# Order of TensorE's stages in a planned kernel: small-tile stages in bundles between token products

## The chip, the cores and the metric

The kernel runs on one core of a Trainium2 chip. The metric is device time in microseconds of one execution, the median of 3 runs. A core has five engines with a queue of their own each: TensorE (PE; its weight loads are shown as PEld), VectorE (DVE), ScalarE (ACT), GpSimd (POOL) and SyncE (SP), which here only issues the DMA transfers. They wait for one another by semaphores, and each works through its own instructions in the order in which the program has them.

## The reference, cut to what matters

Four batches, 8 heads, 576 positions, head size 64, 32 memory slots; all in float32. An attention over a memory is followed by a mixture of 4 experts with given shares, and that by a soft mixture of 8 experts with 4 slots each.

```python
# attention over memory, per batch and head
a = softmax(phi, axis=memory)                    # [576, 32]
k_m, v_m = a.T @ k, a.T @ v                      # [32, 64]
x = softmax(q @ k_m.T / 8) @ v_m                 # [576, 64], heads side by side: [2304, 512]

# first mixture: N 2304, D 512, E 4, F 1024
p = domain_probs / domain_probs.sum(-1)
x = sum(p[:, e:e+1] * (relu(x @ w1[e]) @ w2[e]) for e in range(4))

# second mixture: 8 experts, 32 slots in all
logits = x @ phi2                                # [2304, 32]
d = softmax(logits, axis=0)                      # over all tokens
slot_input = (d.T @ x).reshape(8, 4, 512)
slot_out[e] = relu(slot_input[e] @ v1[e]) @ v2[e]
out = softmax(logits, axis=1) @ slot_out         # [2304, 512]
```

## The kernel before, in words

**What it computes in place of x.** The kernel never makes the attention's output or the first mixture's output. With the 256 attention weights of a token (8 heads, 32 slots) called A, `x @ w1[e]` is `A @ (v_m @ w1[e])`. So for each batch and each chunk of 512 columns of w1 (8 chunks) TensorE makes a table g = v_m @ w1 (`g_mult`, L665 to 691; 16 matmuls at L678, on 64x32 tiles of the array), and then the **token products** (`up`, L735 to 773): h = relu(g.T @ A), one for 128 columns of the chunk and 288 tokens, each of six matmuls (L753 to L755) because g and A are each split into an upper and a lower part. ScalarE takes the relu out of PSUM (L761), VectorE transposes it (L767), GpSimd multiplies by the expert's share (L771).

The logits of the second mixture come from h by way of a table M = w2 @ phi2 (`m_chunk`, L805 to 858, made once, beside the first batch: transposes of w2 at L820, a product with phi2 at L837, a fold at L849). `logits` (L775 to 802) multiplies the four h parts of a chunk by M on 128x32 tiles (L789, in the last two units L796). At the end of a unit of work, `group` (L883 to 1004) turns logits to weights, keeps a running maximum and sum over tokens, and forms the slots' sums d.T @ h on 32x32 tiles (L959), all four PSUM banks at a time.

Meanwhile the next batch is prepared by `attention` (L1138): `memory` (L428; transposes at L447, L451, L466, L540, products at L497, L502, totals at L516, L520) and five `query` blocks (L575; a transpose at L586, ScalarE's copy at L590, the scores at L598, softmax on VectorE, GpSimd and ScalarE, and the parts of A written last at L638 and L640).

**Units.** There are five: batches 0, 1, 2 with 64 token products each, and the two halves of batch 3 with 32 each. After the last, about 40 blocks of 1 MB of w2, v1 and v2 pass through the freed memory: slots' input from the sums (L1187, L1218, L1232), the second mixture (L1261, L1305), the output (L1344).

**What sets the order.** No engine's order is written out by hand. Each stage is put on a list by `Plan.add` with its engine, an estimated cost, what it reads and writes, and a due time `at`. The due time is counted in **places**: one place is one token product (`place`, L699; `starts`, L697). `Plan.order` (L60 to 101) simulates the engines by these costs and always lets an engine take, of the stages whose inputs are ready, the one with the smallest due time:

```python
t = max(free[eng], min(ready[n] for n in cand))
n = min(n for n in cand if ready[n] <= t)
```

The program is then put out in the order found. Which memory and which PSUM bank a stage uses follows from the due times alone, and so does who must wait for whom (`needs`, L28; `Uses.settle`, L145). PSUM has 8 banks: three for token products (`MM`), one for logits (`LB`), two for g and M tables (`g_bank`), two for the next batch (`att_bank`); a group's sums use the last four together. The due times that matter here: token product number p of a unit at p; the g product of the next chunk at 8n + 2.1 for chunk n (4n + 1.1 in the last two units), the logits of chunk n at the start of chunk n + 1 plus 0.6 (the last chunk's: plus 1.6), a query's transpose and scores at 27 + 6i and 29 + 6i, the steps of memory between 6 and 29, a group's first product (L901, L906) 2.4 after the next unit's start and its sums 8.6 after it. The M table's steps are due 4 places apart per chunk from 2.5 on. Six buffers (`NHT`) hold h parts; a chunk's logits read four of them.

Of the kernel before, what the change touches and what calls it, by code (L numbers as in the profile page):

```python
# [8 lines left out]
ALU = mybir.AluOpType  # L9
AX = mybir.AxisListType  # L10


class Plan:

# [1 line left out]

    HOP = 0.1
    RATE = 0.33  # L20

    def __init__(self):
        self.stages = []

    def add(self, eng, cost, fn, r=(), w=(), at=0.0, size=0):
        self.stages.append((at, len(self.stages), eng, cost, fn, tuple(r), tuple(w), size))

    def needs(self, stages):  # L28
        last, readers, spans, needs = {}, {}, [], []
        for n, (_, _, _, _, _, rd, wr, _) in enumerate(stages):  # L30
            need = set()
            for key in rd:
                if key[0] == "W":
                    need.update(m for lo, hi, m, wrote in spans if wrote and lo < key[2] and key[1] < hi)
                elif key in last:
                    need.add(last[key])
            for key in wr:
                if key[0] == "W":
                    need.update(m for lo, hi, m, _ in spans if lo < key[2] and key[1] < hi)
                else:  # L40
                    if key in last:
                        need.add(last[key])
                    need.update(readers.get(key, ()))
            for key in wr:
                if key[0] == "W":
                    spans = [s for s in spans if not (key[1] <= s[0] and s[1] <= key[2])]
                    spans.append((key[1], key[2], n, True))
                else:
                    last[key] = n
                    readers[key] = []  # L50
            for key in rd:
                if key[0] == "W":
                    spans.append((key[1], key[2], n, False))
                else:
                    readers.setdefault(key, []).append(n)
            need.discard(n)
            needs.append(need)
        return needs

    def order(self):  # L60
        stages = sorted(self.stages, key=lambda s: s[:2])
        needs = self.needs(stages)
        after = [[] for _ in stages]
        for n, need in enumerate(needs):
            for m in need:
                after[m].append(n)
        left = [len(need) for need in needs]
        ready = [0.0] * len(stages)
        free, waiting = {}, {}
        for n, s in enumerate(stages):  # L70
            free.setdefault(s[2], 0.0)
            waiting.setdefault(s[2], [])
            if not left[n]:
                waiting[s[2]].append(n)
        line = 0.0
        out = []
        while len(out) < len(stages):
            best = None
            for eng, cand in waiting.items():
                if not cand:  # L80
                    continue
                t = max(free[eng], min(ready[n] for n in cand))
                n = min(n for n in cand if ready[n] <= t)
                if best is None or (t, n) < best[:2]:
                    best = (t, n, eng)
            t, n, eng = best
            waiting[eng].remove(n)
            _, _, _, cost, fn, _, _, size = stages[n]
            free[eng] = t + cost
            end = free[eng] + self.HOP  # L90
            if size:
                line = max(line, free[eng] + 1.2) + size / self.RATE / 1e6
                end = line + 0.6
            out.append((t, n))
            for m in after[n]:
                ready[m] = max(ready[m], end if size or stages[m][2] != eng else free[eng])
                left[m] -= 1
                if not left[m]:
                    waiting[stages[m][2]].append(m)
        self.trace = [(t, stages[n]) for t, n in out]  # L100
        return [stages[n][4] for _, n in out]
# [67 lines left out]
            taken[best[1]].append((a, z, uid))  # L169
        self.found, self.kinds = found, []  # L170


PE, ACT, DVE, POOL, SP = "PE", "ACT", "DVE", "POOL", "SP"


def act(n):
# [143 lines left out]
def program(  # L320
    tc, const, swap, ps, q, k, v, phi, dprob, w1, w2, phi2, v1, v2, out, nc, B, H, S, HD, NM, E, D, F, NSLOT, FH, NCH, SCALE, NT, HB, NG, ident, si, rr, r1, rf, ind, phi2_sb, dp, dps, pe, pe2, ct, kb, vb, kbs, vbs, M, srun, mrun, zrun, small, lts, lrs, lcs, dts, R, RAW, GP, AT, HT, NHT, PH, KT, QB, QT, XB, NX, YB, NY, MX, END, uses, h3, hts, atts, zone, z0, at_place, swapped, bank, MM, LB, S0, plan, **_
):
    add = plan.add

    def wk(o, n):
        return key("W", o, o + n)

    def pk(n):
        return key("ps", n)
# [242 lines left out]
    def a_part(b, x, o, n):  # L572
        return [wk(AT[b % 2] + (2 * c + x) * S + o, n) for c in range(2)]
# [161 lines left out]
    def up(u, n, fb, ki):  # L735
        b, ranges = units[u]
        o0, o1 = ranges[ki]
        base, w = ranges[0][0], o1 - o0
        width = ranges[-1][1] - base
        nt = width // 32  # L740
        e = n // 2
        kx = 4 * (n % 2) + fb
        g, go = G[b * NCH + n]
        f0 = 128 * fb
        bm = mm()
        at = place(u, n, fb, ki)

        def f():
            t = bank[bm][:, 0:w]
            for c in range(2):  # L750
                ah, al = A[b]()[:, c, 0, o0:o1], A[b]()[:, c, 1, o0:o1]
                gh, gl = g()[:, 2 * c, f0:f0 + 128], g()[:, 2 * c + 1, f0:f0 + 128]
                nc.tensor.matmul(t, gh, ah, start=(c == 0), stop=False)  # L753
                nc.tensor.matmul(t, gh, al, start=False, stop=False)  # L754
                nc.tensor.matmul(t, gl, ah, start=False, stop=(c == 1))  # L755
        add(PE, 0.81, f, r=[wk(go, 2048)] + a_part(b, 0, o0, w) + a_part(b, 1, o0, w), w=[pk(bm)], at=at)
        if ki == 0:
            ht_of[u, n, fb] = uses(*[HT + 576 * n for n in range(NHT)])
        ho = ht_of[u, n, fb]
        t = at_place(ho, width)  # L760
        add(ACT, act(w), lambda: nc.scalar.activation(  # L761
            out=t[:, o0 - base:o1 - base], in_=bank[bm][:, 0:w], func=ACTF.Relu,
        ), r=[pk(bm)], w=[wk(ho + o0 - base, w)], at=at + 0.3)
        if ki < len(ranges) - 1:
            return
        hk = wk(h_at(u, e) + 32 * nt * kx, 32 * nt)
        add(DVE, dve(width), lambda: nc.vector.transpose(out=h_of(u, e)[:, kx], in_=t), r=[wk(ho, width)], w=[hk],  # L767
            at=at + 0.4)
        tb0 = base // 32
        share = pe[:, b, tb0:tb0 + nt, e:e + 1].to_broadcast([128, nt, 32])  # L770
        add(POOL, pool(width), lambda: nc.gpsimd.tensor_tensor(  # L771
            out=h_of(u, e)[:, kx], in0=h_of(u, e)[:, kx], in1=share, op=ALU.mult),
            r=["pe"], w=[hk], at=min(at + 10, starts[u + 1] + 1.5))

    def logits(u, n, at):  # L775
        b, ranges = units[u]
        base = ranges[0][0]
        first = n % 2 == 0
        lb = bank[LB]
        hos = [ht_of[u, n, a] for a in range(4)]  # L780

        def f():
            if len(ranges) == 2:
                for h in range(2):
                    for ki, (o0, o1) in enumerate(ranges):
                        for a2 in range(2):
                            a = 2 * h + a2
                            r0 = 64 * ki + 32 * a2
                            nc.tensor.matmul(  # L789
                                lb[r0:r0 + 32, 0:HB], M[:, 4 * n + a, :],  # L790
                                at_place(hos[a] + o0, o1 - o0),
                                start=(first and h == 0), stop=(not first and h == 1),
                            )
            else:
                for a in range(4):
                    nc.tensor.matmul(  # L796
                        lb[32 * a:32 * a + 32, 0:HB], M[:, 4 * n + a, :], at_place(hos[a], HB),
                        start=first, stop=not first,
                    )
        width = ranges[-1][1] - base  # L800
        add(PE, 1.05 * len(ranges) / 2 + 0.05, f,
            r=[("M", n)] + [wk(o, width) for o in hos], w=[pk(LB)], at=at)


    def m_chunk(n, ats):  # L805
# [377 lines left out]
    for e in range(2):  # L1183
        def turn_s(e=e):
# [6 lines left out]
            at=z + 0.1)  # L1191
        x = sts[:, e]
        src = bank[so_b[e]].rearrange("p (k s) -> p k s", k=8)
        w = [("M", n) for n in range(NCH)] if e == 0 else [("sts", 1)]
        if e:
            add(DVE, dve(512), lambda x=x, src=src: nc.vector.tensor_copy(out=x, in_=src), r=[pk(so_b[e])] + [("M", 7)],
                w=[("sts", e)], at=z + 0.2)
        else:
            add(ACT, act(512), lambda x=x, src=src: nc.scalar.copy(out=x, in_=src), r=[pk(so_b[e])],
                w=[("sts", e)] + [("M", n) for n in range(NCH)], at=z + 0.2)  # L1200
# [11 lines left out]
    for n in range(8):  # L1212
        t, tk = blk[loads[n]]
# [36 lines left out]
    for m in range(4):  # L1250
        bu = end_mm()
        zz = z + 3 + 2 * m
        for n in range(4):
            ep, ch = divmod(n, 2)
            t, tk = blk[1, 2 * m + ep, ch]
# [42 lines left out]
    for e in range(8):  # L1298
        for nn in range(2):
            t, tk = blk[2, e, nn]  # L1300
# [8 lines left out]
            at = zz + 0.1 * (2 * e + nn)  # L1309
# [7 lines left out]
    for n, ab in enumerate(accs):  # L1317
        so, sk = sos[n]
        at = zz + 0.75 + n
        add(ACT, act(256), lambda ab=ab, so=so: nc.scalar.copy(out=so[:, 0:256], in_=bank[ab][:, 0:256]),  # L1320
            r=[pk(ab)], w=[("so", n, 0), sk], at=at)
# [9 lines left out]
        w=[("so4", 0)] + keys, at=zz + 2)  # L1331
# [23 lines left out]
    at = zz + 3  # L1355
# [52 lines left out]
```

## Time and profile before

| What | Value |
|---|---|
| Time, median of 3 runs | 517.08 us (516.25 to 517.65) |
| Profiled execution, device time | 517.01 us |
| Its span, first to last instruction | 515.2 us |
| TensorE busy | 485.4 us (94%), 5592 matmuls |
| VectorE, ScalarE, GpSimd busy | 302.0, 201.8, 211.2 us |
| Transfers | 106.08 MB, 206 GB/s over the span |
| Mean granted TensorE clock | 0.99 |
| Token matmuls (L753, L754, L755) | 512 each, of 316, 295 and 295 ns |
| g products (L678), logits (L789, L796) | 512 matmuls; 384 and 128 matmuls |

A view's busy time says when an engine had an instruction under way. For TensorE the ends are modelled and matmuls overlap, so a matmul of 295 ns can be followed by the next one 130 ns later: what a matmul costs in a row of others is the distance between their starts. The first token product starts at 30.05 us, the last unit's ends at about 420 us; before that the first inputs are loaded and prepared, after it come the last sums and the second mixture.

### The profile page before, as it was taken

The numbers are of one execution on the slowest core, as the hardware profiler recorded it, in microseconds if no ns is written. First come the engines' busy times: TensorE is split into PE (matmuls) and PEld (weight loads), VectorE is DVE, ScalarE is ACT, GpSimd is POOL, SyncE is SP. The second block draws the span as 40 slices with busy tenths as digits, with TensorE's granted clock in tenths as the row PEclk, the third lists the DMA queues.
The fourth block names the chain that finished last, engine by engine and source line by source line (L and its number), as shares of the span: only waits on it lengthen the run. The fifth ranks groups of instructions, "written<-read, shape, count | busy, mean of one in ns | idle before, by whom it ended". The sixth has DMA issues, their size and how long they took to land.

```text
span 515.2 us, 13206 instructions
## 1 busy us (share of the span) xinstructions
PE 485.4 (94%) x5592; PEld 340.1 (66%) x5592; DVE 302.0 (59%) x605; ACT 201.8 (39%) x475; POOL 211.2 (41%) x255
## 2 busy tenths in 40 slices
PE   4999999999999999999999999999999998999971
PEld 2677887877876788777678887756676876333230
DVE  6488544767685758767684777675557553200032
ACT  2354444545541545555154554533443430011021
POOL 0244412547650448774234777622664860000000
PEclk9999999999999999999999999999999999899997
DMA  7999758333520855334072652824425988999938
GB/s 224 231 346 324 295 170 238 111 96 103 180 85 19 271 173 150 104 112 156 3 248 85 188 178 94 282 88 132 156 83 188 384 268 326 415 424 422 417 130 334
DMA packets 65243, 106.08 MB, mean 206 GB/s; under 512 B 28576, under 2 KB 40864, under 8 KB 59552
## 3 DMA queue, kind: packets, MB, share of 16 engines
q1 hardware_dynamic: 65184, 105.23, 60.2%
q8 instruction: 44, 0.72, 0.6%
q14 instruction: 15, 0.12, 0.1%
HBM read 100.50 MB, written 4.72 MB: 204 GB/s over the span
## 4 chain that ended last, share of the span: by engine, by line
PE 77%; DMA 14%; SPq 3%; DVE 2%; ACT 1%; issue 1%; DVEq 0%; ACTq 0%
PE ps L753 16%; PE ps L755 13%; PE ps L754 13%; PE ps L959 8%; DMA v<-in_moe_w_dram 8%; PE ps L678 6%; PE ps L789 5%; DMA h<-in_moe_w_dram 3%; PE ps L820 3%; SPq L351 3%; DMA raw<-in_moe_w_dram 3%; PE ps L796 2%; PE ps L598 2%; PE ps L837 1%; PE ps L849 1%; PE ps L586 1%
## 5 line engine op out<-in xcount | busy, mean ns | idle before, releaser
L771 POOL TENSOR_TENSOR h<-h,pe 128x576 f32<-128x576 f32 (+1 forms) x160 | 156.9, 991 | 165.1 <-DVE h L767 120.2
L761 ACT ACTIVATE hts<-ps 128x288 f32<-128x288 f32 x256 | 105.4, 412 | 156.1 <-PE ps L755 154.7
L753 PE MATMUL ps<-A,g 128*128 128x288 f32 x512 | 161.8, 316 | 0.1
L755 PE MATMUL ps<-A,g 128*128 128x288 f32 x512 | 151.3, 295 | 0.2 <-DVE g L689 0.2
L754 PE MATMUL ps<-A,g 128*128 128x288 f32 x512 | 151.0, 295 | 0.0
L767 DVE STREAM_TRANSPOSE h<-hts 128x576 f32<-128x576 f32 (+1 forms) x160 | 102.5, 649 | 52.7 <-ACT hts L761 52.2
L753 PEld LDWEIGHTS ps<-A,g 128*128 128x128 f32 x512 | 96.1, 188 | 38.0 <-issue 26.9
L755 PEld LDWEIGHTS ps<-A,g 128*128 128x128 f32 x512 | 96.1, 188 | 0.8 <-DVE g L689 0.8
L754 PEld LDWEIGHTS ps<-A,g 128*128 128x128 f32 x512 | 96.3, 188 | 0.2 <-POOL A L640 0.2
L689 DVE TENSOR_TENSOR g<-ps,g 128x512 fp32r<-128x512 f32 x64 | 40.9, 680 | 19.2 <-ACT g L687 19.1
L687 ACT CAST g<-ps 128x512 fp32r<-128x512 f32 x64 | 34.5, 589 | 20.1 <-PE ps L678 19.3
L959 PE MATMUL ps<-h,dts 32*32 32x512 f32 x1152 | 40.0, 597 | 1.6 <-DVE dts L941 1.6
L678 PE MATMUL ps<-raw,vbs 64*32 64x512 f32 x512 | 35.3, 601 | 0.6 <-DMA raw<-in_moe_w_dram 0.6
L959 PEld LDWEIGHTS ps<-h,dts 32*32 32x32 f32 x1152 | 22.8, 103 | 15.2 <-issue 4.7
L789 PE MATMUL ps<-hts,M 128*32 128x288 f32 x384 | 28.3, 412 | 0.0
L615 POOL TENSOR_TENSOR atts<-atts,small 128x256 f32<-128x256 f32 (+1 forms) x20 | 11.5, 573 | 25.7 <-DVE small L613 25.5
L820 PE MATMUL ps<-ident,h 128*128 128x128 f32 x128 | 18.5, 276 | 0.0
L826 DVE COPY h<-ps 128x512 f32<-128x512 f32 x16 | 11.1, 691 | 10.1 <-PE ps L820 10.0
L789 PEld LDWEIGHTS ps<-hts,M 128*32 128x32 f32 x384 | 10.0, 109 | 10.0 <-issue 4.5
L640 POOL TENSOR_TENSOR A<-atts,A 128x256 fp32r<-128x256 f32 (+1 forms) x20 | 13.6, 680 | 5.5 <-ACT A L638 5.2
L820 PEld LDWEIGHTS ps<-ident,h 128*128 128x128 f32 x128 | 14.9, 144 | 0.9 <-DVE small L457 0.5
L626 POOL TENSOR_TENSOR atts<-atts,small 128x256 f32<-128x256 f32 (+1 forms) x20 | 11.5, 573 | 8.5 <-DVE small L624 6.1
(185 smaller groups left out, 515.6 us busy)
## 6 DMA issues: line engine op xcount, KB each, us to landing
raw<-in_moe_w_dram SPq DMA_DIRECT2D x32, 1024.0 KB, 5.2
v<-in_moe_w_dram SPq DMA_DIRECT2D x20, 1024.0 KB, 11.9
h<-in_moe_w_dram SPq DMA_DIRECT2D x18, 1024.0 KB, 8.2
h<-in_k_dram SPq DMA_DIRECT2D x8, 512.0 KB, 5.3
h<-in_v_dram SPq DMA_DIRECT2D x8, 512.0 KB, 6.7
atts<-in_moe_w_dram SPq DMA_DIRECT2D x4, 1024.0 KB, 8.3
atts<-in_q_dram SPq DMA_DIRECT2D x12, 256.0 KB, 5.7
atts<-in_phi_dram SPq DMA_DIRECT2D x8, 256.0 KB, 3.6
```

The source lines that it names most:

```text
L678: nc.tensor.matmul(bank[bs[c]][32 * i:32 * i + 32, :], vb[b % 2][64 * c:64 * c + 64, 32 * i:32 * i + 32], t()[64 * c:64 * c + 64, i, :], s ...
L687: add(ACT, act(512), lambda c=c, src=src: nc.scalar.copy(out=placed(g()[:, 2 * c]), in_=src), r=[pk(bs[c])], w=[wk(o + 1024 * c, 512)], at ...
L689: add(DVE, dve(512), lambda c=c, src=src: nc.vector.tensor_tensor(out=placed(g()[:, 2 * c + 1]), in0=src, in1=placed(g()[:, 2 * c].bitcast ...
L753: nc.tensor.matmul(t, gh, ah, start=(c == 0), stop=False)
L754: nc.tensor.matmul(t, gh, al, start=False, stop=False)
L755: nc.tensor.matmul(t, gl, ah, start=False, stop=(c == 1))
L761: add(ACT, act(w), lambda: nc.scalar.activation(out=t[:, o0 - base:o1 - base], in_=bank[bm][:, 0:w], func=ACTF.Relu,), r=[pk(bm)], w=[wk(h ...
L767: add(DVE, dve(width), lambda: nc.vector.transpose(out=h_of(u, e)[:, kx], in_=t), r=[wk(ho, width)], w=[hk], at=at + 0.4)
L771: add(POOL, pool(width), lambda: nc.gpsimd.tensor_tensor(out=h_of(u, e)[:, kx], in0=h_of(u, e)[:, kx], in1=share, op=ALU.mult), r=["pe"], ...
L789: nc.tensor.matmul(lb[r0:r0 + 32, 0:HB], M[:, 4 * n + a, :], at_place(hos[a] + o0, o1 - o0), start=(first and h == 0), stop=(not first and ...
L820: nc.tensor.transpose(bank[bk][:, 128 * c:128 * c + 128], wn()[:, a, 128 * c:128 * c + 128], ident)
L959: nc.tensor.matmul(bank[S0 + p][32 * c:32 * c + 32, :], dtv[rows, tb, :], h_pair(u, ep)[rows, :, :, tb, :], start=(tb < 2), stop=(tb >= nt ...
```

## The change

The planner gets a second rule for TensorE. Each stage has a `lag`: None for token products, 0 for logits, 1 (`LAG`) for all others. Of the ready stages, the planner looks at the first token product a and the first other stage b. If TensorE's last stage was a token product, b is taken only when it is due at least `lag` places before a. If TensorE's last stage was another, b is taken as long as it is due at most 8 places (`AHEAD`) after a. Also, the simulated cost of a TensorE stage grows by 0.15 (`TURN`) when it is of the other sort than the stage before. Stages of other engines have no None among them, and are chosen as before. What reads what, the due times, the memory and the banks are unchanged, and so are all instructions.

```diff
@@ -9,8 +9,13 @@
 ALU = mybir.AluOpType
 AX = mybir.AxisListType
 
+PE, ACT, DVE, POOL, SP = "PE", "ACT", "DVE", "POOL", "SP"
+
 
 class Plan:
+
+
+
 
 
 
@@ -18,16 +23,18 @@
 
     HOP = 0.1
     RATE = 0.33
+    LAG, AHEAD = 1, 8
+    TURN = 0.15
 
     def __init__(self):
         self.stages = []
 
-    def add(self, eng, cost, fn, r=(), w=(), at=0.0, size=0):
-        self.stages.append((at, len(self.stages), eng, cost, fn, tuple(r), tuple(w), size))
+    def add(self, eng, cost, fn, r=(), w=(), at=0.0, size=0, lag=LAG):
+        self.stages.append((at, len(self.stages), eng, cost, fn, tuple(r), tuple(w), size, lag))
 
     def needs(self, stages):
         last, readers, spans, needs = {}, {}, [], []
-        for n, (_, _, _, _, _, rd, wr, _) in enumerate(stages):
+        for n, (_, _, _, _, _, rd, wr, _, _) in enumerate(stages):
             need = set()
             for key in rd:
                 if key[0] == "W":
@@ -72,7 +79,16 @@
             waiting.setdefault(s[2], [])
             if not left[n]:
                 waiting[s[2]].append(n)
-        line = 0.0
+        line, tokens = 0.0, False
+
+        def first(cand, t):
+            cand = [n for n in cand if ready[n] <= t]
+            a = min((n for n in cand if stages[n][8] is None), default=None)
+            b = min((n for n in cand if stages[n][8] is not None), default=None)
+            if a is None or b is None:
+                return b if a is None else a
+            gap = stages[a][0] - stages[b][0]
+            return b if gap >= (stages[b][8] if tokens else -self.AHEAD) else a
         out = []
         while len(out) < len(stages):
             best = None
@@ -80,12 +96,15 @@
                 if not cand:
                     continue
                 t = max(free[eng], min(ready[n] for n in cand))
-                n = min(n for n in cand if ready[n] <= t)
+                n = first(cand, t)
                 if best is None or (t, n) < best[:2]:
                     best = (t, n, eng)
             t, n, eng = best
             waiting[eng].remove(n)
-            _, _, _, cost, fn, _, _, size = stages[n]
+            _, _, _, cost, fn, _, _, size, lag = stages[n]
+            if eng == PE:
+                cost += self.TURN * (tokens != (lag is None))
+                tokens = lag is None
             free[eng] = t + cost
             end = free[eng] + self.HOP
             if size:
@@ -170,8 +189,6 @@
         self.found, self.kinds = found, []
 
 
-PE, ACT, DVE, POOL, SP = "PE", "ACT", "DVE", "POOL", "SP"
-
 
 def act(n):
     return 0.17 + 0.00083 * n
@@ -753,7 +770,7 @@
                 nc.tensor.matmul(t, gh, ah, start=(c == 0), stop=False)
                 nc.tensor.matmul(t, gh, al, start=False, stop=False)
                 nc.tensor.matmul(t, gl, ah, start=False, stop=(c == 1))
-        add(PE, 0.81, f, r=[wk(go, 2048)] + a_part(b, 0, o0, w) + a_part(b, 1, o0, w), w=[pk(bm)], at=at)
+        add(PE, 0.81, f, r=[wk(go, 2048)] + a_part(b, 0, o0, w) + a_part(b, 1, o0, w), w=[pk(bm)], at=at, lag=None)
         if ki == 0:
             ht_of[u, n, fb] = uses(*[HT + 576 * n for n in range(NHT)])
         ho = ht_of[u, n, fb]
@@ -799,7 +816,7 @@
                     )
         width = ranges[-1][1] - base
         add(PE, 1.05 * len(ranges) / 2 + 0.05, f,
-            r=[("M", n)] + [wk(o, width) for o in hos], w=[pk(LB)], at=at)
+            r=[("M", n)] + [wk(o, width) for o in hos], w=[pk(LB)], at=at, lag=0)
 
 
     def m_chunk(n, ats):
```

## Rows read from the trace of the kernel before

**Rows 1.** The page, its head and part 1: busy us (share) xinstructions.
```profile
span 515.2 us, 13206 instructions
...
PE 485.4 (94%) x5592; PEld 340.1 (66%) x5592; DVE 302.0 (59%) x605; ACT 201.8 (39%) x475; POOL 211.2 (41%) x255
```

**Rows 2.** Busy time by stretch: length, busy per engine, granted clock, DMA share, GB/s.
```profile
30.00:141.00 111.00, 110.86 (x1149) 87.69 (x1149) 72.82 (x142) 55.41 (x127) 50.63 (x56) 1.00 0.64 197
141.00:234.00 93.00, 92.63 (x1214) 71.27 (x1213) 65.63 (x116) 43.65 (x107) 50.69 (x54) 1.00 0.45 139
...
326.50:382.00 55.50, 55.08 (x671) 35.66 (x669) 34.66 (x70) 22.30 (x52) 25.86 (x39) 1.00 0.45 149
...
431.50:441.00 9.50, 8.87 (x81) 6.09 (x84) 6.06 (x16) 1.03 (x2) 0.00 (x0) 1.00 0.85 329
441.00:494.50 53.50, 49.58 (x339) 16.85 (x332) 3.29 (x13) 3.71 (x6) 0.00 (x0) 0.97 0.97 403
```

**Rows 3.** TensorE's timeline, second unit: start us, us, engine, line, tiles, shape, count.
```profile
194.67 0.29 PE L754 MATMUL ps<-A,g 128*128 128x288 f32 x1
194.80 0.29 PE L755 MATMUL ps<-A,g 128*128 128x288 f32 x1
195.02 1.18 PE L789 MATMUL ps<-hts,M 128*32 128x288 f32 x16
196.13 0.66 PE L586 MATMUL ps<-ident,atts 128*128 128x128 f32 x4
196.54 0.38 PE L753 MATMUL ps<-A,g 128*128 128x288 f32 x1
196.76 0.30 PE L754 MATMUL ps<-A,g 128*128 128x288 f32 x1
...
198.31 1.09 PE L678 MATMUL ps<-raw,vbs 64*32 64x512 f32 x16
199.33 0.67 PE L598 MATMUL ps<-atts,kbs 128*32 128x128 f32 x16
199.92 0.40 PE L753 MATMUL ps<-A,g 128*128 128x288 f32 x1
```

**Rows 4.** The same timeline where g product and logits stand together, at 328 us.
```profile
328.24 1.09 PE L678 MATMUL ps<-raw,vbs 64*32 64x512 f32 x16
329.26 1.18 PE L789 MATMUL ps<-hts,M 128*32 128x288 f32 x16
330.36 0.40 PE L753 MATMUL ps<-A,g 128*128 128x288 f32 x1
```

**Rows 5.** The same timeline: first and last of the excursions between token products.
```profile
32.88 0.44 PE L1111 MATMUL ps<-dp,rr 32*128 32x72 f32 x2
...
416.82 0.69 PE L796 MATMUL ps<-hts,M 128*32 128x288 f32 x8
417.44 0.41 PE L753 MATMUL ps<-A,g 128*128 128x288 f32 x1
```

**Rows 6.** Timeline of all engines at 366 us; in brackets idle before, and releaser.
```profile
366.08 1.24 PE L796 MATMUL ps<-hts,M 128*32 128x288 f32 x8
366.19 0.41 ACT L761 ACTIVATE hts<-ps 128x288 f32<-128x288 f32 x1 [0.33 <-PE ps L755]
...
366.65 0.14 PEld L796 LDWEIGHTS ps<-hts,M 128*32 128x32 f32 x2 [0.42 <-ACT hts L761]
...
367.26 0.40 PE L753 MATMUL ps<-A,g 128*128 128x288 f32 x1
```

**Rows 7.** Timelines of GpSimd and TensorE at the second unit's end.
```profile
229.17 0.46 POOL L640 TENSOR_TENSOR A<-atts,A 128x128 fp32r<-128x128 f32 x1 [0.75 <-ACT A L638]
...
233.77 0.29 PE L753 MATMUL ps<-A,g 128*128 128x288 f32 x1
```

**Rows 8.** Timeline of the DMA queue, and the chain that ended last.
```profile
431.65 2.54 SPq L351 DMA_DIRECT2D h<-in_moe_w_dram  x5
...
476.92 17.52 DMA h<-in_moe_w_dram
```

## The prediction

> **What bounds the kernel now.** I read the page first, for the busy shares: TensorE is busy for 485.4 of a span of 515.2 us [rows 1]. A mean over the span hides stages, so next came the busy time by stretches [rows 2]. From 30 to 382 us the PE column fills each stretch (110.86 of 111.00, 92.63 of 93.00, 55.08 of 55.50, and the stretch from 234 is like that from 141), with the DMA engines at about half and the granted clock at 1.00, the higher of the two levels, throughout. From 441 to 494.5 us it is the transfers: DMA share 0.97 at 403 GB/s. So one limit holds up to the last group's sums, and another after them.
>
> The third view is TensorE's timeline, because "busy" there has modelled ends. What counts is the distance between starts [rows 3]. Inside a token product the starts stand 0.13 us apart (194.67, 194.80). Where a stage of another kind follows, the last token matmul takes 0.22 (194.80 to 195.02), and the first one on the way back takes 0.22 to 0.24 (196.54 to 196.76). Each excursion from tokens to small-tile work and back thus costs 0.09 + 0.10 = 0.19 us beside its own work, though no view calls it idle. From the first to the last there are 112 such excursions between tokens [rows 5]: 40 up to 141 us, 25 in each of the next two units, 14 to 382 us, 8 after that. This is what a change of order can save.
>
> The fourth view is the timeline of all engines around one logits stage in the fourth unit [rows 6], which shows a wait inside a "busy" stretch: the last LDWEIGHTS of the stage start at 366.65, when ScalarE's relu (366.19, 0.41 us) is done. The stage takes 366.08 to 367.26, 1.18 us; the same stage without the wait takes 0.62 (416.82 to 417.44) [rows 5]. So 0.56 us is lost. Four logits stages between 360 and 378 us have this form.
>
> **The change part by part.** No instruction is added or removed: 5592 matmuls before and after. DMA, ScalarE, VectorE and GpSimd stages all carry the default lag, for them the new choice is the old one (lowest number that is ready). They move only because the planned times move. I put that at zero, with one microsecond on either side.
>
> *Logits and g products.* Before, a g product (due two token products, or in the last two units one, after its chunk began) and the logits of the chunk before (due 0.6 after the chunk began) stand as two excursions with a token product between. Logits keep their old moment (lag 0). Now, with TensorE in the small work, the g product, due at most 1.5 places ahead, follows at once. Its banks and its raw weights are free by then in all chunks but the one behind the group's sums. In the trace the two are apart 7 + 8 + 8 + 5 = 28 times and together twice. What the pair costs when together stands in one place [rows 4]: L678 from 328.24 to 329.26 is 1.02 us, L789 from 329.26 to 330.36 is 1.10, which is what each takes singly (1.11 and 1.02 in rows 3). Nothing is lost inside, a whole excursion goes: 28 x 0.19 = 5.3 us.
>
> Here a rule speaks against the change. The row first: two forms of tile, 64*32 and 128*32, side by side in 1.02 + 1.10 us [rows 4]. The Trainium skill (TensorEngine Tiling (Array Packing), section Key Properties) says that a change of tiling mode, not only of the tile, drains the engine. By that rule the change of form inside the pair would cost as well: three changes stay of four, and the 28 pairs would give 28 x 0.19 / 2 = 2.7 us. The row disagrees for this pair, so the sum goes by the row; the rule's case is in rival B.
>
> *Other small stages.* Scores (L598), memory products (L497), the M table (L837) and the group's first product (L901) are taken in the same bundles if ready and due within eight places. L598 behind L678 takes 199.33 to 199.92, 0.59 us [rows 3], so one merged also saves 0.19. Of the 89 excursions with a small-tile stage, 61 are left after the pairs. Many are tied: a score needs its query's transpose and ScalarE's copy first, the M table has only two banks, the sums (four banks) shut out all that comes after them. From none to all is 0 to 11.6 us; I take 5 in the first unit and 4 in each of the next two, 13 x 0.19 = 2.5 us. Transposes (L586, L820) have the tokens' form 128*128 and take 0.41 in a bundle [rows 3]; moving them I count at nothing.
>
> *The waits of unit four.* There the order has been: two tokens, g product, two tokens, logits, and the logits come right behind the chunk's last token, since the next chunk's g is not yet cast when the plan looks. With the g product beside the previous logits, three tokens (18 matmuls at 0.13, 2.4 us) lie between it and the next chunk instead of two, so the next token is ready and covers the relu. Four times 0.56 is 2.2 us; around the sums the same stretch holds a logits stage and a late g that cost more, of which I take 0.6. Bounds: nothing (the wait stays) to 4.5 us. Sum taken: 2.8.
>
> *What is delayed.* Any stage but logits may wait until it is one place (0.8 us) overdue. The cover is the slack in the chain that prepares the next batch: its last part is written at 229.17 + 0.46, the first token that needs it starts at 233.77, so 4.1 us are spare [rows 7]. Two places late cost nothing; past five, each place costs 0.8 us in each of three batches. Bundling ahead makes most of that chain earlier, so I take zero.
>
> *Waits that the bundles bring.* TensorE works in order. If a score stands in the bundle right behind the work that covers its ScalarE copy, and the copy is later than planned, all tokens behind it wait. Nearest row: 0.56 us for a relu met too early [rows 6]. 15 scores of three batches at between 0 and 0.56 is 0 to 8.4 us. The plan's cost of such a copy is close to the trace's, so I take 0.13 each, nearer the low end: 2.0 us back.
>
> *Does it reach the end?* After the sums, five loads are issued at 431.65 [rows 8], the moment that TensorE frees their memory; the DMA share before and after that is 0.85, so the queue was not behind. From there a chain of transfers runs, the last for 17.52 us from 476.92. It starts with TensorE and is as long as before; what TensorE gains before 382 us arrives whole. Between 382 and 420 us nothing is paired, I count zero.
>
> *Sum.* -5.3 - 2.5 - 2.8 + 2.0 = -8.6 us. The profiled execution took 517.01 us (the span of 515.2 and 1.8 around it), the median shown is 517.08, so no correction: 508.5 us.
>
> **The rivals.**
>
> *B: half of it.* Changes of form inside a bundle cost like those at its edges, and the fourth unit's logits still meet the relu. Then the 5.3 and the 2.5 are halved to 2.7 and 1.3, none comes from the waits, nothing goes back: 517.0 - 4.0 = 513 us. (The Trainium skill's rule on tiling modes, above, is this case.) For it: only two pairs stand together in the trace. Against: rows 4.
>
> *C: slower, by bundles that block.* Place: small stages that depend on one another inside a bundle, with tokens ready behind them. There are about 73 candidates (15 scores, six steps of memory in each of three batches, some 40 of the M tables). At the price of rows 6, 0.56 us, it decides from 10.6 / 0.56 = 19 stages on; with 24 of them stalled, 13.4 - 10.6 = 3 us slower, 520 us. For it: TensorE already met late operands unseen. Against: the planner takes a stage only when its operands are due by its own durations.
>
> *D: no change, the transfers hold the end.* If the last loads could not come earlier, 8.6 us would be lost again before 441 us: 517 us. For it: 403 GB/s from 441 us on. Against: rows 8, the loads are released by TensorE. The same time comes if the planner finds hardly any stage ready early, so that the order stays.
>
> **How the numbers follow.** The forecast has 0.64, B 0.19, D 0.09, C 0.08. The likeliest gives 508.5, its own range is 504.5 to 512. A range of 504.5 to 515.0 takes in B and leaves out D, C and a few hundredths below. Changes under 0.3% (1.55 us) can't be told from none here. Faster: the forecast and B, 0.83; same 0.09; slower 0.08.
>
> **What would show it.** In TensorE's timeline of after, L789 and L678 stand side by side, with some 60 to 75 excursions for 112; the token runs between are longer, eight products in units two and three. L796 takes 0.62, not 1.18. The stretch up to the first unit's end is 2 us shorter, the next two about 2, the fourth 3 to 4; the last 133 us from 382 are the same. Wrong it would be if the excursions fall but the stretches don't (B or C: look for L598 or L497 with LDWEIGHTS that wait for ACT), or if a DMA load stands in the chain before 420 us.

## The result, and the profile after

The changed kernel takes 509.03 us (median of 4, 507.71 to 510.28) where the kernel before takes 517.12. The ratio is 0.984, its 95% interval 0.982 to 0.985: 1.6% or 8.1 us faster. Taken again beside the last experiments it had 510.32 us and a ratio of 0.988 (0.986 to 0.990). Predicted were 508.5 us, in a range of 504.5 to 515.0.

The page's head and part 1, as in [rows 1]:

```profile
span 505.9 us, 13222 instructions
...
PE 476.3 (94%) x5592; PEld 338.2 (67%) x5592; DVE 297.1 (59%) x605; ACT 202.7 (40%) x475; POOL 212.1 (42%) x255
```

The same 5592 matmuls, 9.1 us less in which one is under way; the sums of ScalarE and GpSimd differ by 0.9 us, and VectorE's is 4.9 us lower. Busy time by stretch answers to [rows 2]; the stretches are units one, two, four and five (of the five with 64, 64, 64, 32 and 32 token products):

```profile
29.20:140.00 110.80, 110.44 (x1155) 87.56 (x1152) 71.90 (x142) 56.42 (x127) 51.31 (x56) 1.00 0.64 202
140.00:230.00 90.00, 90.00 (x1211) 70.56 (x1210) 63.91 (x115) 43.54 (x106) 50.31 (x53) 1.00 0.46 141
...
320.50:372.30 51.80, 50.73 (x670) 34.64 (x669) 34.62 (x70) 22.36 (x52) 26.21 (x38) 1.00 0.41 135
372.30:410.80 38.50, 38.50 (x406) 30.42 (x404) 24.39 (x56) 14.51 (x37) 25.53 (x40) 1.00 0.68 246
```

With the units' ends taken from the timeline (start of a unit's last token matmul), their lengths are these, for the kernels that matter below. The last two rows divide the time from the first to the last token matmul by steps, a step being the distance from one TensorE start to the next: those that begin at a token matmul, and those that begin in any other stage.

| us | before | after | after, again | price only (e1) | forms (e10) | mixed (e11) | single (e5) | lag 8 (e7) |
|---|---|---|---|---|---|---|---|---|
| first token starts | 30.05 | 29.35 | 29.76 | 31.21 | 31.61 | 29.92 | 29.59 | 30.68 |
| unit one | 111.1 | 110.5 | 111.3 | 112.8 | 113.5 | 115.3 | 116.7 | 117.2 |
| unit two | 92.5 | 90.0 | 90.0 | 92.6 | 89.9 | 90.9 | 96.2 | 93.7 |
| unit three | 92.8 | 90.5 | 90.5 | 92.4 | 90.4 | 91.3 | 96.3 | 92.2 |
| unit four | 55.4 | 51.8 | 51.8 | 53.1 | 51.8 | 51.8 | 58.5 | 52.4 |
| unit five | 38.0 | 38.4 | 38.4 | 38.0 | 38.4 | 38.4 | 39.7 | 39.3 |
| excursions | 112 | 71 | 71 | 114 | 67 | 67 | 142 | 49 |
| token steps | 222.7 | 217.0 | 217.8 | 224.3 | 215.3 | 216.3 | 230.0 | 213.3 |
| other steps | 167.0 | 164.3 | 164.3 | 164.6 | 168.7 | 171.4 | 177.5 | 181.5 |

So 0.6 us come from unit one, 2.5 and 2.3 from the next two, 3.6 from unit four, and 0.5 are lost in unit five: 8.5 us in all, 5.8 of them in token steps. (The two profiled spans differ by 9.3 us, because the first token also starts 0.7 us earlier.) The two profiles of the changed kernel agree to 0.1 us from unit two on; what differs is the start and unit one, where a transpose (L837) waited 1.2 us for a load of w2 in the second profile. Whether that is why the two medians differ by 1.3 us is not shown, since one execution of each was profiled.

TensorE's timeline of a bundle in unit two (columns as in [rows 3]):

```profile
202.50 1.18 PE L806 MATMUL ps<-hts,M 128*32 128x288 f32 x16
203.49 0.66 PE L615 MATMUL ps<-atts,kbs 128*32 128x128 f32 x16
204.08 1.09 PE L695 MATMUL ps<-raw,vbs 64*32 64x512 f32 x16
205.10 0.66 PE L603 MATMUL ps<-ident,atts 128*128 128x128 f32 x4
205.51 0.38 PE L770 MATMUL ps<-A,g 128*128 128x288 f32 x1
```

Logits, scores, g product and a query's transpose were up to four excursions before; here they are one of 3.01 us. The logits take 0.99 us with scores behind them; in [rows 3] they take 1.11, with a transpose behind. What stands behind matters between two small forms as well, as a bundle 9 us later shows:

```profile
211.26 0.66 PE L615 MATMUL ps<-atts,kbs 128*32 128x128 f32 x16
211.73 1.17 PE L806 MATMUL ps<-hts,M 128*32 128x288 f32 x16
212.83 1.09 PE L695 MATMUL ps<-raw,vbs 64*32 64x512 f32 x16
```

Scores take 0.47 us with logits behind them, of the same form; with a g product behind, on 64*32, they take 0.59 above, as they do with a token behind in [rows 3]. Logits take 1.10 us with a g product behind. So in both stages a change of form behind costs 0.11 to 0.12 us, to 64*32 as much as to 128*128. Transposes have the tokens' form. Between tokens they cost only their own work, as here before the change:

```profile
203.07 0.29 PE L755 MATMUL ps<-A,g 128*128 128x288 f32 x1
203.21 0.60 PE L586 MATMUL ps<-ident,atts 128*128 128x128 f32 x4
203.56 0.38 PE L753 MATMUL ps<-A,g 128*128 128x288 f32 x1
203.78 0.30 PE L754 MATMUL ps<-A,g 128*128 128x288 f32 x1
```

From 203.07 to 203.78 us pass 0.71 us: two token steps of 0.13 and four transposes, which start 0.11 apart. Of the 112 excursions before, 23 hold only stages of this form, mostly transposes, of the 71 after 9; so those with small tiles fell from 89 to 62.

In unit four, the place that answers to [rows 6]:

```profile
364.24 0.69 PE L813 MATMUL ps<-hts,M 128*32 128x288 f32 x8
364.86 1.09 PE L695 MATMUL ps<-raw,vbs 64*32 64x512 f32 x16
365.88 0.40 PE L770 MATMUL ps<-A,g 128*128 128x288 f32 x1
```

The logits take 0.62 us, not 1.18, and the g product stands right behind them. The tail, as in [rows 8], from the DMA queue and the chain:

```profile
422.43 2.59 SPq L368 DMA_DIRECT2D h<-in_moe_w_dram  x5
...
467.74 17.36 DMA h<-in_moe_w_dram
```

The five loads are issued 9.2 us earlier, the last transfers begin 9.2 us earlier, and these take as long as before (17.36 for 17.52).

### The profile page after: what moved, and what is told of

Its sections match the earlier page's. It is cut to its first block, busy times and chain, and to the rows that moved or that the text cites. A ratio compares the mean times of both kernels' runs of the same rounds, so it can differ in the third digit from the quotient of the medians.

```text
span 505.9 us, 13222 instructions
## 1 busy us (share of the span) xinstructions
PE 476.3 (94%) x5592; PEld 338.2 (67%) x5592; DVE 297.1 (59%) x605; ACT 202.7 (40%) x475; POOL 212.1 (42%) x255
## 4 chain that ended last, share of the span: by engine, by line
PE 78%; DMA 14%; SPq 3%; DVE 2%; ACT 1%; issue 1%; DVEq 0%; ACTq 0%
PE ps L770 15%; PE ps L771 13%; PE ps L772 13%; PE ps L976 8%; DMA v<-in_moe_w_dram 8%; PE ps L695 6%; PE ps L806 5%; DMA h<-in_moe_w_dram 3%; PE ps L837 3%; SPq L368 3%; DMA raw<-in_moe_w_dram 3%; PE ps L813 2%; PE ps L854 2%; PE ps L603 2%; PE ps L615 2%; PE ps L866 1%
## 5 line engine op out<-in xcount | busy, mean ns | idle before, releaser
L770 PE MATMUL ps<-A,g 128*128 128x288 f32 x512 | 158.0, 309 | 0.2 <-ACT hts L778 0.2
L770 PEld LDWEIGHTS ps<-A,g 128*128 128x128 f32 x512 | 96.1, 188 | 23.9 <-issue 18.6
L771 PEld LDWEIGHTS ps<-A,g 128*128 128x128 f32 x512 | 96.2, 188 | 0.3 <-POOL A L657 0.2
L837 PE MATMUL ps<-ident,h 128*128 128x128 f32 x128 | 18.1, 278 | 0.2 <-DVE g L706 0.2
L837 PEld LDWEIGHTS ps<-ident,h 128*128 128x128 f32 x128 | 14.5, 143 | 2.4 <-issue 1.4
L894 POOL TENSOR_TENSOR lts<-lts,pe 128x288 f32<-128x288 f32 x15 | 10.4, 691 | 12.6 <-DMA v<-in_moe_w_dram 9.4
```

The lines of the kernel that those rows point to most:

```text
L837: nc.tensor.transpose(bank[bk][:, 128 * c:128 * c + 128], wn()[:, a, 128 * c:128 * c + 128], ident)
```

## The experiments

Each was timed against the kernel before, which stood at 517.4, 517.2 and 517.0 us beside them. They change only the planner's choice, so the work is the same in all.

**e1, the planned price alone.** The old choice, TURN kept:

```diff
-            return b if gap >= (stages[b][8] if tokens else -self.AHEAD) else a
+            return min(a, b)
```

> The old choice (smallest due time first) is back, only the planned price of a change of sort (0.15) stays. 114 excursions from token products, before 112. My theory (what counts is how many excursions there are, 0.19 us each, and the waits of the fourth unit): no change, 517 us, within 1 us. Rival (the gain comes from a plan whose times are nearer to the chip's, so that fewer stages meet late operands): at least 3 us faster, 511 to 514 us.

Measured: 516.54 us, ratio 0.999 (0.997 to 1.000), no change in sum. But the units show two effects that cancel: unit one 1.7 us longer than before, unit four 2.3 us shorter. In unit four the logits now stand behind the third token of a group of three, and the wait of [rows 6] is gone without any bundle:

```profile
363.60 0.69 PE L813 MATMUL ps<-hts,M 128*32 128x288 f32 x8
364.22 0.40 PE L770 MATMUL ps<-A,g 128*128 128x288 f32 x1
```

From this kernel to the changed one, the first four units lose 2.3, 2.6, 1.9 and 1.3 us: 8.1 us; the token steps of all five lose 7.3. For 43 excursions that is 0.19 each, but only on average, since 16 of the 43 hold nothing but stages of the tokens' form.

**e2, only ahead.**

```diff
-    LAG, AHEAD = 1, 8
+    LAG, AHEAD = 0, 8
```

> Stages are not held back (lag 0 for all), but in small work TensorE goes on for up to eight places ahead. 76 excursions, the whole change has 71. My theory: 5 excursions x 0.19 = 1 us less gain than the whole change, 510 us. Rival (holding stages back until one place late is what makes the bundles): 514 us or more.

Measured: 510.20 us, 0.987 (0.985 to 0.988). Going on in small work makes the bundles; holding back is worth a microsecond at most, since the changed kernel had 0.984 in one set of runs and 0.988 in another.

**e3, from the fourth unit on, and e4, before it.**

```diff
+            if stages[a][0] < 192:      # e4: >= 192
+                return min(a, b)
```

> The new choice only from the fourth unit on (token products due from place 192). Excursions 14 to 8 in that unit, the others about as before. My theory (six excursions and waits of relu on top): 6 x 0.19 + 2.5 = 3.6 us, 513.5 us. Rival (only the excursions count): 1.1 us, 516 us.

> The new choice only in the first three units; from the fourth on the old one (15 excursions there). My theory: the three units keep what the trace after shows, 0.6 + 2.5 + 2.3 = 5.4 us, 511.5 us; together with the kernel that has it only from the fourth unit on it adds up to the whole change (8.1 us). Rival (units depend on one another, for instance through transfers): the two parts don't add up, by 2 us or more.

Measured: e3 515.34 us, 0.996 (0.995 to 0.998); e4 510.06 us, 0.986 (0.984 to 0.988). They miss my numbers by 1.8 and 1.4 us, and the sum, 2.0 + 7.3 = 9.4 us, is over the whole change's 8.1. The units tell why: both keep the planned price, which lengthens unit one in e3 (112.9 us) and shortens unit four in e4 (53.1). In e3 unit four is 51.8 us, and in e4 the first three units are 110.6, 90.0 and 90.5 us, as in the changed kernel. So no tie between the units shows beside the price.

**e5, the opposite dose.**

```diff
-            return b if gap >= (stages[b][8] if tokens else -self.AHEAD) else a
+            return b if tokens and gap >= stages[b][8] else a
```

> Opposite dose: in small work a token product is taken whenever one is ready, so an excursion holds one stage, mostly. 142 excursions, the kernel with only the planned price of a change of sort has 114. My theory (0.19 us for each excursion, whatever is in it): 28 x 0.19 = 5.3 us slower than that kernel, 522 us. Rival (a change of tile form costs wherever it stands, in a bundle or at its edge): about half, 519 us. Rival (waits for late operands decide): no slope, 515 to 518 us, since stages that depend on one another never stand side by side here.

Measured: 535.57 us, 1.034 (1.031 to 1.037). Slower, as both theories with a slope say, but by 19 us where 5 were expected. In units two and three the 21 further excursions go with 7.4 us, half of it (3.8) in token steps. In the whole kernel the token steps are 5.7 us longer than e1's, the other steps 12.8. Before the LDWEIGHTS of L770 its queue stood idle for 30.3 us until ScalarE's relu in this trace, for 6.9 before the change; so this kernel changed waits too, and its slope is no price of an excursion. What makes up the 12.8 us is left open.

**e6, bundles without the planned price.**

```diff
-    TURN = 0.15
+    TURN = 0.0
```

> The whole change without the planned price of a change of sort (TURN 0). 74 excursions for 71. With the price alone the first unit was 1.7 us longer and the fourth 2.3 us shorter than before. My theory (the fourth unit's waits go once g product and logits stand together, with or without that price; the first unit's extra waits come from it): first unit about 109.5 us, fourth about 52, whole 508 us. Rival (the price is what moved the logits behind a token): the fourth unit's waits are back, 54 us or more there, whole 510 to 511 us.

Measured: 509.02 us, 0.984 (0.981 to 0.988), the changed kernel's time. Unit four:

```profile
321.60:373.10 51.50, 51.50 (x670) 35.02 (x669) 34.53 (x70) 22.25 (x52) 26.30 (x38) 1.00 0.40 135
```

So the pair removes that unit's waits by itself, as e1's price does by itself: two ways to one gain, which is had once. Unit one is 110.5 us, not the 109.5 that I expected: with bundles, no effect of the price shows there.

**e7 and e8, longer bundles.**

```diff
-    LAG, AHEAD = 1, 8
+    LAG, AHEAD = 8, 16      # e8: 4, 16
```

> Bundles as long as they get: up to eight places behind, up to sixteen ahead (logits as before). 49 excursions for 71. My theory as long as nothing is late: 22 x 0.19 = 4.2 us faster than the changed kernel, 505 us. Rival (stages held back eight places make the next batch's A late, 4.1 us of slack, or block in bundles): 509 us or more, with a token product that waits for GpSimd's A or with LDWEIGHTS that wait for ACT.

> Between the two: up to four places behind, up to sixteen ahead. 63 excursions for 71. My theory: 8 x 0.19 = 1.5 us faster than the changed kernel, 507.5 us. Rival (holding back costs more than an excursion): 509 us or more.

Measured: e7 522.34 us, 1.010 (1.006 to 1.014), slower than before with the fewest excursions of all; e8 515.16 us, 0.996 (0.994 to 0.999). The waits of e7's TensorE (us in total, times, longest), the three that the kernel after has in a smaller size (1.4 us of the first lie before the first token in both):

```profile
PE ps L514 <- ACT atts L496: 4.3, 3, 1.4
PE ps L695 <- DVE g L706: 2.7, 3, 1.4
PE ps L837 <- DVE g L706: 2.3, 2, 1.4
```

and its unit one:

```profile
30.50:148.00 117.50, 111.93 (x1157) 87.94 (x1151) 71.16 (x140) 55.55 (x127) 50.52 (x55) 1.00 0.62 187
```

TensorE stands still for 5.6 us there (117.50 - 111.93). For 3.7 of them it waits in a bundle for VectorE to empty the banks of a g product, because the next g product or the M table's transposes want the same two banks; for 1.7 two steps of the M table (L854, L866) wait for their operands. In the changed kernel the first two of these waits are 1.7 and 0.9 us, the third 0.2.

**e9 to e11, what inside a bundle costs.** In e10 and e11 the transposes and the M table's fold carry a mark, `full` says whether TensorE's last stage had it, and among the ready stages (due within eight places) one form goes first, the same or the other:

```diff
-            return b if gap >= (stages[b][8] if tokens else -self.AHEAD) else a
+            if gap < (stages[b][8] if tokens else -self.AHEAD):
+                return a
+            near = [n for n in cand if stages[n][8] is not None
+                    and stages[a][0] - stages[n][0] >= -self.AHEAD]
+            same = [n for n in near
+                    if (stages[n][8] == 1.001) == (tokens or full)]   # e11: (not tokens and not full)
+            return min(same or [b])
```

> The changed kernel once more, on the same chip as the three below, as their measure. Both theories: 509 us, within 1.

> The change with one more rule: within a bundle, a stage of the form that TensorE has (128*128 as the token products and transposes, or small tiles) goes first among the ready ones due within eight places. 67 excursions, and 120 changes between the full form and small tiles, the changed kernel has 71 and 136. Theory 1 (an excursion costs 0.19 us, whatever is inside): 4 x 0.19 = 0.8 us faster than the changed kernel, the same as the kernel with forms mixed. Theory 2 (each change of form costs half of that, 0.095 us, wherever it stands): 16 x 0.095 = 1.5 us faster than the changed kernel, 507.5 us, and 32 x 0.095 = 3.0 us faster than the mixed one.

> The opposite: within a bundle the other form goes first. Also 67 excursions, but 152 changes of form, 32 more than with forms kept together. Theory 1 (excursions): the same as that kernel, within 0.5 us. Theory 2 (each change of form, 0.095 us): 3.0 us slower than that kernel, 1.5 us slower than the changed one, 510.5 us.

Measured: e9 510.32, e10 512.53 (ratio 0.991, 0.990 to 0.993), e11 515.88 us (0.997, 0.996 to 0.999). Forms mixed cost 3.35 us more than forms together, with 67 excursions in both, so the number of excursions is not all that is paid. There are 32 more changes between the full form and small tiles, if the 64*128 transposes of the last query block count as full, as their mark says: 0.105 us each. (By the tile forms in the trace there are 30.)

Units two and three (89.9 and 90.4 us in e10, 90.9 and 91.3 in e11) hold 1.9 us of it, for 18 more such changes, or for 15 more changes of any form (93 for 78): 0.10 to 0.13 each. Against the changed kernel the two ways of counting differ: in these units e10 has 8 changes fewer between the full form and small tiles, but only 3 fewer of any form, and it is 0.2 us shorter there, not 0.8. So a change from one small form to another is paid too, as the lines at 211 us show. e10 is nevertheless 2.2 us slower than the changed kernel, not 1.5 faster: unit one loses 2 to 3 us. TensorE waits there 2.3 us for VectorE to empty the banks of g products, in the changed kernel 0.2.

**e12, a later plan.**

```diff
-    HOP = 0.1
+    HOP = 0.2
```

> The change with a planned delay of 0.2 for 0.1 between an engine's end and another's start, so that the plan takes dependent stages later. 71 excursions as in the changed kernel. Theory (waits of small stages for operands that the plan thought ready still cost some 1.5 us in the first and 1.5 in the fourth unit): up to 2 us faster, 507 us. Rival (these waits come from shared banks, not from the planned delay): no change, 509 us.

Measured: 514.63 us, 0.996 (0.994 to 0.997): slower than the changed kernel by 4 us, which neither case said. Unit four gains 0.5 us (51.4), unit one is 114.1 us long; TensorE waits there 1.4 us for VectorE to empty the banks of a g product. No kernel tried is clearly faster than the changed one; e6, e4 and e2 equal it within their noise.

## Why the prediction was right, point by point

*The bound and the tail* held. TensorE is busy nearly throughout units one to five (110.44 of 110.80 us, 50.73 of 51.80), and from the last token matmul to the end the spans have 95.4 us before and 95.3 after. Rival D is out.

*Fewer excursions*: -5.3 and -2.5 for 28 pairs and 13 other stages, 41 in all. They fell from 112 to 71, by 41, but that these numbers agree is luck. Only 19 bundles hold both logits and g product where I had counted on 30, and 14 of the 41 held only stages of the tokens' own form, mostly transposes, on which nothing is saved; 27 held small tiles. In unit one it was 5 of 11, and instead of 2 us that unit became 0.6 us shorter in one profile and 0.2 longer in the other. The price at the edges was right: steps from a token into small tiles fell from 72 to 51, first token steps behind small tiles from 78 to 42. At the 0.09 and 0.10 us of [rows 3] that is 1.9 + 3.6 = 5.5 us, and the token steps are 5.8 us shorter. So the term of 7.8 was 2 us too large.

*Changes inside a bundle* I held to be free, because the pair of [rows 4] takes what its stages take singly. That row can't show it: the single times have a change of form behind them too (the g product's 1.02 us scores on 128*32, the logits' 1.11 a transpose). With scores of their own form behind them, logits take 0.11 us less. A pair still saves its whole 0.19 us at the tokens, because the change behind each of its stages is paid in either order; where transposes or g products part stages of one form, it is paid again.

Here the rule that I set aside was nearer than my reading of the row. The Trainium skill (TensorEngine Tiling (Array Packing), section Key Properties) says that a change of tiling mode, not only of the tile, drains the engine. The 0.11 to 0.12 us behind logits and scores, for either other form, agree with that; a drain itself no run shows. So rival B's premise was right, while its 513 us was not, since a merge saves both edges at the tokens even where the change inside stays.

*The waits of unit four*: -2.8 predicted. Five logits stages took 1.18 to 1.65 us there before, 3.3 us more than their 0.62; after, all take 0.62 but one. e1 has the unit 2.3 us shorter by the planned price alone, e6 has the waits gone without it. The mechanism (a third token between g product and logits) is what both traces show; that the price would do it too I had not seen.

*Waits that bundles bring*: 2.0 predicted, in the scores of later batches. No score waits there. The one of any size is in unit four, where a g product right behind logits stands idle for 0.9 us until VectorE has emptied its banks; the others are of 0.2 and 0.3 us. That such waits can eat everything was rival C; e7 shows it at 522 us: token steps 3.7 us shorter than in the changed kernel, other steps 17.2 us longer. Its places are not the scores, though, but the two banks that g products and the M table share (5.0 us), and memory products that wait for ScalarE (2.9 us in units two and three).

So the mechanism was right, but that 8.6 us came out so close (8.1 by the medians, 8.5 from the first to the last token) is in part luck: the excursions brought less than planned, and the new waits took less.

*Unit five*, put at zero, lost 0.5 us: the final group's first product (L923) now stands before the last three token products; of that the tail gives 0.1 back. *Delays* cost nothing, as assumed: units two and three start without a gap.

## What to carry to other kernels

Where an engine is full, look at the distance between starts at each change of kind: here 0.19 us that no view called idle came 89 times, and order alone took 27 of them out. Bundle work of one form, but only until the bundle's stages want the same buffers: past that point a merge brings a wait (up to 1.4 us in e7) that is several times the 0.19 it saves. And when a gain has two causes in one change (here the new choice and the planned price), run each alone before adding their terms.

## What the runs showed that was not expected

A change of form is paid between two small forms as well: logits with a g product behind them (64*32) take 0.11 us longer than with scores (128*32), just as with a token or a transpose. And what a stage takes "singly" already holds the change behind it, so two stages side by side that take as long as singly do not show that the change is free. Unit one, in which g products and the M table share two banks, took 111.1 us before, and 1 to 6 us more under most other orders (112.3 in e2 to 117.2 in e7, one profile of each); the changed kernel (110.5 and 111.3), e4 and e6 did not.
